# Moving the magnitude of six w_out pieces to ScalarE and the low part of w_sg to GpSimd

## The chip, the cores and the metric

The kernel runs on one core of one Trainium2 chip. Its time is what the device takes for one execution, in microseconds (us); lower is better. One core has five engines that run side by side, each through a queue of its own, in the order fixed when the program is built: TensorE (PE, the matmuls; its weight loads are shown as PEld), VectorE (DVE), ScalarE (ACT), GpSimd (POOL) and SyncE (SP, which here issues nearly all DMAs). An instruction that waits holds up everything behind it in its queue.

## The reference

Three layers follow one another, for 4 batches of 576 rows and 512 columns:

```
scores = q k^T / 8 + slope_h * -(|i - j|), kept where 0 <= i - j < 128;  x = softmax(scores) v   (8 heads of 64)
h = gelu(x @ w_in);  u, v = halves of h
v_n = (v - mean) / sqrt(var + 1e-6) * g_ln
x2 = x + (u * (w_sg @ v_n + b_sg)) @ w_out            (w_sg is 576 x 576, over the rows; w_out 512 x 512)
h = relu(x2 @ w_in2); c = convolution of h over 3 rows; out = (h * sigmoid(c)) @ w_out2
```

Some inputs (w_in, w_out, w_in2, w_out2, the convolution's weights) come as 64-bit floats, w_sg as 32-bit floats.

## The kernel before, in words

Every matmul of the dense layers is made of three: each operand is split into a high part (the value cast to the matmul's own format) and a low part (the value minus the high part), and high x high, high x low and low x high are summed in PSUM. So each weight is prepared in SBUF before it is used.

A 64-bit weight is first turned into 32 bits by whole-number work in `narrowed` (L310). The load brings pairs of words. For a piece of 128 x 256 numbers the steps are: the magnitude of the high word into a tile `wa` (on VectorE a bitwise AND at L324, or on ScalarE the activation Abs at L322, chosen by the argument `act_abs`), a clamp (L328), mask and shift (L329), the sign and top bits (L330), and the bits of the low word (L331), all but the first always on VectorE. Then `split` (L244) makes the high part with `copy` and the low part with `tt`, a subtraction; the table `ON` (L41) names the engines for each kind of operand. For w_out ("wo") the high part is a cast on ScalarE (L222) and the low part a subtraction on GpSimd (L231). There are two `wa` buffers for these pieces, so the third piece starts when the low part of the first is done. The eight pieces are the steps `o0.0` to `o3.1` (function `w_out_piece`, L373).

w_sg comes as five pieces of 128 x 576, steps `g0` to `g4` (function `w_sg_piece`, L363): a cast on ScalarE (L222, "w32 hi") and a subtraction ("w32 lo", L231). Pieces of both kinds are loaded by `staged` (L358) into tiles of a ring of eight buffers with the tag "x"; a load into a used buffer waits until its last reader is done.

The order of the steps is written out by hand (`_steps`, L57). Around the change the first batch's dense layer is woven with the attention of the second batch, whose four head pairs are called p4 to p7 here: `C` scores (matmuls into PSUM, then nine fused bias-and-minimum instructions on VectorE, L451, tile t), `E` exponentials on ScalarE (L186, nine for each pair), `N` the scaling by 1/sum (L242, VectorE or GpSimd; the reciprocal at L498 and L499), `T` transposes on TensorE (L515, tile pT) and their copies to SBUF (tile ph, L222 or L224), `A` the product with v (tile o). Of the dense layer `V` makes v (psv, its statistics at L781 to L786, the vn tiles), `U` makes u (psu), `G` multiplies by w_sg (pss), scales and adds on VectorE (L843), multiplies by u on GpSimd (L231, tile t) and splits the result into gh and gl, and `W` multiplies by w_out (pso). The scores of p4, p5 and p6 and all of `U` come before the first `G`. Six PSUM banks serve the attention; one pair's scores take five.

Some operations may go to one of several engines. A planner decides at build time, in the order of the steps: `load` holds booked nanoseconds of each engine, `book` adds to it, and `pick` takes the engine with the lowest sum; an engine's sum is never lower than 6000 ns behind TensorE's (L39, L202). The costs that it books are those in `copy`, `tt` and `scaled` (L215 to L242). `narrowed` books the same on VectorE whichever engine takes the magnitude. Behind the planner, the framework places each engine's instructions in an order of its own, from the priorities of the steps and a model of their times.

Of the kernel before, what the change touches and what calls it, by code (L numbers as in the profile page):

```python
# [38 lines left out]
SLACK = 6000.0  # L39

ON = {  # L41
    "clamp": "dve", "win hi": "act", "win lo": "pool", "win u hi": "dve", "win u lo": "pool", "w64 hi": "pool", "w64 lo": "pool", "w32 hi": "act", "wo hi": "act", "wo lo": "pool", "w32 lo": "dve",
    "norm": "dve pool",
    "x hi": "act pool", "x lo": "dve", "x first hi": "act", "x first lo": "pool", "x late hi": "act", "x late lo": "dve", "vn first hi": "act", "vn first lo": "dve", "vn hi": "pool", "vn lo": "dve",
    "gate": "pool", "g hi": "act dve pool", "g lo": "dve pool", "x2 hi": "act pool", "x2 lo": "dve",
# [89 lines left out]
def attention_gmlp_glu_kernel(  # L135
# [24 lines left out]
    def f(ap):  # L160
        return ap.bitcast(F32)
# [39 lines left out]
    def book(eng, ns):  # L201
        load[eng] = max(load[eng], load["pe"] - SLACK) + ns  # L202

    def pick(costs):
        eng = min(costs, key=lambda e: max(load[e], load["pe"] - SLACK) + costs[e])
        book(eng, costs[eng])
        return eng
# [36 lines left out]
    def split(hi, lo, src, kind=None, done=None):  # L244

        ins = copy(hi, src, kind is None, ON[kind + " hi"] if kind else "act dve")
        if done is not None:
            done[:] = [ins.ins.name]
        return tt(lo, src, f(hi), ALU.subtract, ON[kind + " lo"] if kind else "dve")
# [9 lines left out]
    with tc.using_default_side("right"):  # L259
        pa = ExitStack()  # L260
        apool = pa.enter_context(tc.tile_pool(name="apool", bufs=2))
# [27 lines left out]
    for i in range(NP):  # L289
        st = cpool.tile([P, 18], F32, name=f"st{i}")  # L290
# [19 lines left out]
    def narrowed(src, n, pool, tag, bufs, spool, stag, sbufs, act_abs=False):  # L310

        if spool is None:
            st = src
        else:
            st = spool.tile([P, STAGE[stag]], U32, tag=stag, name="w64", bufs=sbufs)
            dma = nc.sync.dma_start(st[:, : 2 * n], src)
            later(dma)
        words = st[:, : 2 * n].rearrange("p (n w) -> p n w", w=2)
        low, high = words[:, :, 0], words[:, :, 1]
        a = pool.tile([P, 256 if tag == "wa" else 512], U32, tag=tag, name="wa", bufs=bufs)[:, :n]  # L320
        if act_abs:
            tc.keep_in_program_order(nc.scalar.activation(f(a), f(high), AF.Abs))  # L322
        else:
            ins = tc.keep_in_program_order(nc.vector.tensor_scalar(a, high, 0x7FFFFFFF, None, op0=ALU.bitwise_and))  # L324
            if last_hi:
                tc.add_manual_dep(ins.ins, last_hi[-1], follow, reason="high part first")
        clamp = nc.gpsimd if pick({e: c for e, c in dict(dve=67 + 0.52 * n, pool=147 + 0.93 * n).items() if e in ON["clamp"]}) == "pool" else nc.vector
        tc.keep_in_program_order(clamp.tensor_scalar(f(a), f(a), W_LOW, W_HIGH, op0=ALU.max, op1=ALU.min))  # L328
        nc.vector.tensor_scalar(a, a, 0x07FFFFFF, 3, op0=ALU.bitwise_and, op1=ALU.logical_shift_left)  # L329
        nc.vector.scalar_tensor_tensor(a, high, 0xC0000000, a, op0=ALU.bitwise_and, op1=ALU.bitwise_or)  # L330
        nc.vector.scalar_tensor_tensor(a, low, 29, a, op0=ALU.logical_shift_right, op1=ALU.bitwise_or)  # L331
        book("dve", 200 + 2.6 * n)
        return f(a)

    def cols(w, k, c0, n):

        return w.bitcast(U32)[:, k, 2 * c0 : 2 * (c0 + n)]

    w64, last_in, last_win, last_hi = {}, [], [], []

    def later(dma):

        tc.add_manual_dep(dma.ins, last_in[0].ins.name, follow, reason="later")
# [14 lines left out]
    def staged(src, dtype):  # L358
        st = mpool.tile([P, S], dtype, tag="x", name="wst", bufs=8)[:, : src.shape[-1]]
        later(nc.sync.dma_start(st, src))  # L360
        return st
# [11 lines left out]
    def w_out_piece(k, half):  # L373
        if k == half == 0:
            kept["wo"] = w1pool.tile([P, NK, 2, 2, 256], F32R, tag="wo", name="wo")
        st = staged(cols(w_out, k, half * 256, 256), U32)
        a = narrowed(st, 256, apool, "wa", 2, None, "x", 8)
        split(kept["wo"][:, k, half, 0, :], kept["wo"][:, k, half, 1, :], a, "wo")

    p2pool = []  # L380
# [491 lines left out]
    def constants(i):  # L872
# [11 lines left out]
        B=rotations,  # L884
        k=constants, l=z_load, v=z_vload, c=z_scores, e=z_exp, n=z_norm, t=z_transpose, z=z_av, j=w_in_load, L=a_load, M=a_vload, C=a_scores, E=a_exp, N=a_norm, T=a_transpose, A=a_av,
        X=a_xsplit, V=m_v, U=m_u, G=m_sg, W=m_wo, i=w_in_piece, g=w_sg_piece, o=w_out_piece, a=w2_piece,
    )

# [230 lines left out]
```

## Time and profile before

| what | value |
|---|---|
| median of 3 runs | 543.01 us (542.52 to 544.82) |
| the profiled execution's own time | 543.29 us |
| its span, first to last instruction | 541.1 us |
| matrix multiplies and weight loads (PE, PEld) | 520.7 us and 474.7 us busy |
| VectorE, ScalarE, GpSimd busy | 367.7, 258.7 and 243.2 us |
| granted TensorE clock, mean | 0.997 |

The profile is of one execution, and 2.2 us of its time lie outside the span. Busy time of an engine is summed over its instructions; what is left of the span is idle, and each idle stretch is put down to the instruction that ended it (its releaser). Matmuls are pipelined, so a busy TensorE can still be slowed. The granted clock is a share of full speed: 1.00 is 2.4 GHz and 0.50 is 1.2 GHz.

### The profile page before, as it was taken

The numbers are of one execution on the slowest core, as the hardware profiler recorded it, in microseconds if no ns is written. First come the engines' busy times: TensorE is split into PE (matmuls) and PEld (weight loads), VectorE is DVE, ScalarE is ACT, GpSimd is POOL, SyncE is SP. The second block draws the span as 40 slices with busy tenths as digits, with TensorE's granted clock in tenths as the row PEclk, the third lists the DMA queues.
The fourth block names the chain that finished last, engine by engine and source line by source line (L and its number), as shares of the span: only waits on it lengthen the run. The fifth ranks groups of instructions, "written<-read, shape, count | busy, mean of one in ns | idle before, by whom it ended". The sixth has DMA issues, their size and how long they took to land.

```text
span 541.1 us, 11980 instructions
## 1 busy us (share of the span) xinstructions
PE 520.7 (96%) x4548; PEld 474.7 (88%) x4548; DVE 367.7 (68%) x959; ACT 258.7 (48%) x673; POOL 243.2 (45%) x383
## 2 busy tenths in 40 slices
PE   8997989999998999999999999999999999999997
PEld 6776879898898988989988999998998999999887
DVE  4999798754878875879767688687567354654300
ACT  6694578342458451376534434452554333444310
POOL 2444238542146363246453344245586545465500
PEclk9999989999999999999999999999999999999999
DMA  8974541433261765243643433902202100100011
GB/s 290 394 241 175 150 121 52 148 113 98 89 201 37 218 187 190 82 124 92 173 144 115 155 101 131 337 13 52 75 21 81 66 22 19 42 21 27 33 39 59
DMA packets 33209, 63.93 MB, mean 118 GB/s; under 512 B 3968, under 2 KB 13952, under 8 KB 33152
## 3 DMA queue, kind: packets, MB, share of 16 engines
q1 hardware_dynamic: 33008, 63.04, 35.8%
q8 instruction: 36, 0.59, 0.5%
q14 instruction: 21, 0.17, 0.1%
q10 hardware_dynamic: 144, 0.13, 0.1%
HBM read 48.47 MB, written 14.68 MB: 117 GB/s over the span
## 4 chain that ended last, share of the span: by engine, by line
PE 62%; DVE 14%; ACT 9%; POOL 7%; DMA 5%; issue 3%; SPq 0%; ACTq 0%; DVEq 0%; POOLq 0%
PE psg L213 31%; PE psv L213 7%; PE pso L213 6%; PE psu L213 5%; PE o L213 4%; ACT t L186 3%; PE pss L213 3%; PE sc L213 3%; POOL t L242 3%; PE pT L515 2%; DMA w<-in_w_in_dram 2%; DVE t L451 1%; DVE wa L330 1%; DMA kq<-in_qk_dram 1%; DVE wa L328 1%
## 5 line engine op out<-in xcount | busy, mean ns | idle before, releaser
L213 PEld LDWEIGHTS psg<-x2g,w 128*128 128x128 f32 x768 | 103.1, 188 | 2.4 <-ACT hb L973 0.7
L213 PE MATMUL psg<-x2g,w 128*128 128x256 f32 (+1 forms) x768 | 104.6, 294 | 0.6 <-ACT hb L973 0.5
L213 PE MATMUL psg<-wout,gh 128*128 128x512 f32 (+1 forms) x272 | 80.1, 378 | 0.0
L186 ACT ACTIVATE t<-t,st 128x192 f32<-128x192 f32 (+1 forms) x144 | 61.9, 431 | 15.0 <-DVE st L451 15.0
L213 PE MATMUL pss<-wsg,vn 128*128 128x256 f32 (+1 forms) x448 | 63.6, 298 | 3.6 <-DVE t L843 3.0
L213 PEld LDWEIGHTS pss<-wsg,vn 128*128 128x128 f32 x448 | 60.5, 190 | 4.7 <-DVE t L843 4.0
L977 DVE SCALAR_TENSOR_TENSOR cc<-hb,cw,cc 128x576 f32<-128x576 f32 x32 | 26.6, 832 | 46.9 <-POOL cc L242 46.9
L213 PEld LDWEIGHTS psg<-wout,gh 128*128 128x128 f32 x272 | 49.8, 188 | 8.7
L213 PE MATMUL psu<-xg,win 128*128 128x320 f32 (+1 forms) x384 | 54.2, 298 | 2.6 <-ACT win L222 1.7
L213 PEld LDWEIGHTS psu<-xg,win 128*128 128x128 f32 x384 | 51.7, 188 | 3.7 <-ACT win L222 1.8
L213 PE MATMUL pso<-gh,wo 128*128 128x256 f32 (+1 forms) x256 | 51.8, 300 | 0.5 <-DVE t L843 0.5
L213 PE MATMUL psg<-wout,gl 128*128 128x512 f32 (+1 forms) x136 | 50.9, 378 | 0.0
L213 PE MATMUL psv<-win,xg 128*128 128x512 f32 x192 | 47.6, 398 | 0.9 <-DVE wa L328 0.9
L242 POOL TENSOR_SCALAR cc<-hb,cw 128x576 f32<-128x576 f32 x32 | 28.3, 885 | 42.7 <-ACT hb L973 42.7
L451 DVE CUSTOM_DVE_ANT_0 t<-sc,tab 128x192 f32<-128x192 f32 (+1 forms) x144 | 40.4, 335 | 5.4 <-PE sc L213 5.0
L973 ACT ACTIVATE hb<-psg 128x576 f32<-128x576 f32 x32 | 20.7, 651 | 47.5 <-PE psg L213 45.0
L213 PEld LDWEIGHTS psv<-win,xg 128*128 128x128 f32 x192 | 35.5, 188 | 8.7 <-ACT win L222 1.0
L231 DVE TENSOR_TENSOR gg<-cc,hb 128x576 f32<-128x576 f32 x32 | 30.1, 943 | 17.2 <-ACT cc L186 17.0
L213 PEld LDWEIGHTS pso<-gh,wo 128*128 128x128 f32 x256 | 40.3, 188 | 1.7 <-DVE t L843 1.2
L213 PE MATMUL pso<-gl,wo 128*128 128x256 f32 (+1 forms) x128 | 36.9, 301 | 1.3 <-POOL gl L231 0.6
L231 POOL TENSOR_TENSOR t<-t,u 128x256 f32<-128x256 f32 (+1 forms) x32 | 27.2, 854 | 18.6 <-DVE t L843 18.4
L231 POOL TENSOR_TENSOR gl<-gg,gh 128x512 fp32r<-128x512 f32 x24 | 33.7, 1404 | 0.6
(101 smaller groups left out, 960.4 us busy)
## 6 DMA issues: line engine op xcount, KB each, us to landing
V<-in_v_dram SPq DMA_DIRECT2D x12, 704.0 KB, 4.7
x2s<-x2d SPq DMA_DIRECT2D x16, 288.0 KB, 2.9
w<-in_w_in_dram SPq DMA_DIRECT2D x8, 512.0 KB, 7.5
w<-in_w_out_dram SPq DMA_DIRECT2D x16, 256.0 KB, 3.2
w<-in_w_in_dram SPq DMA_DIRECT2D x16, 256.0 KB, 2.8
wout<-w2d SPq DMA_DIRECT2D x8, 512.0 KB, 6.0
q<-in_q_dram SPq DMA_DIRECT2D x12, 320.0 KB, 4.0
out_dram<-ot SPq DMA_DIRECT2D x15, 256.0 KB, 2.0
```

The costliest lines, as they stand in the source:

```text
L186: ins = nc.scalar.activation(*args, **kw)
L213: return nc.tensor.matmul(out, lhsT, rhs, start=start, stop=stop, **kw)
L231: return (nc.vector if eng == "dve" else nc.gpsimd).tensor_tensor(dst, a, b, op=op)
L242: e.tensor_scalar(dst, src, col, 1.0, op0=ALU.mult, op1=ALU.mult)
L328: tc.keep_in_program_order(clamp.tensor_scalar(f(a), f(a), W_LOW, W_HIGH, op0=ALU.max, op1=ALU.min))
L330: nc.vector.scalar_tensor_tensor(a, high, 0xC0000000, a, op0=ALU.bitwise_and, op1=ALU.bitwise_or)
L451: nc.vector.tensor_tensor_reduce(e, bank, table, scale=-SCALE, scalar=3e38, op0=ALU.add, op1=ALU.min, accum_out=mx)
L515: ins = nc.tensor.transpose(ps[:, i * P : (i + 1) * P], src, ident)
L973: nc.scalar.activation(h[:, 1 : S + 1], ps[:, 256 : 256 + S], AF.Relu)
L977: nc.vector.scalar_tensor_tensor(cc, h[:, 0:S], cw[:, 0, c : c + 1], cc, op0=ALU.mult, op1=ALU.add)
```

## The change

The low parts of the five w_sg pieces are subtracted on GpSimd in place of VectorE, and for the first six of the eight w_out pieces the magnitude is the activation Abs on ScalarE in place of the bitwise AND on VectorE. Nothing else in the source differs; what the planner books for w_sg's low part follows the engine (L229).

```diff
 ON = {
-    ... "wo hi": "act", "wo lo": "pool", "w32 lo": "dve",
+    ... "wo hi": "act", "wo lo": "pool", "w32 lo": "pool",
...
     def w_out_piece(k, half):
...
         st = staged(cols(w_out, k, half * 256, 256), U32)
-        a = narrowed(st, 256, apool, "wa", 2, None, "x", 8)
+        a = narrowed(st, 256, apool, "wa", 2, None, "x", 8, 2 * k + half < 6)
         split(kept["wo"][:, k, half, 0, :], kept["wo"][:, k, half, 1, :], a, "wo")
```

## Rows read from the trace of the kernel before

**Rows 1.** The page's first part: busy us, share of the span, instructions.
```profile
PE 520.7 (96%) x4548; PEld 474.7 (88%) x4548; DVE 367.7 (68%) x959; ACT 258.7 (48%) x673; POOL 243.2 (45%) x383
```
**Rows 2.** Waits of TensorE, 65 to 130 us: total us, times, longest.
```profile
PE sc L213 <- DVE st L451: 2.1, 1, 2.1
PE pso L213 <- POOL gl L231: 0.6, 2, 0.3
```
**Rows 3.** Timeline of TensorE: start, us, line, operation, count [idle before <-releaser].
```profile
50.88 0.38 PE L213 MATMUL psu<-xg,win 128*128 128x256 f32 x1 [1.71 <-ACT win L222]
...
76.77 2.49 PE L213 MATMUL sc<-k,q 64*64 64x192 f32 x24 [2.09 <-DVE st L451]
78.80 10.24 PE L213 MATMUL pss<-wsg,vn 128*128 128x256 f32 x70
88.88 1.58 PE L515 MATMUL pT<-ident,t 128*128 128x128 f32 x13
...
92.44 2.05 PE L213 MATMUL o<-ph,V 128*64 128x64 f32 x52
```
**Rows 4.** Busy us by stretch: PE, PEld, DVE, ACT, POOL, granted clock, DMA.
```profile
50.00:55.00 5.00, 4.12 (x23) 3.63 (x24) 4.35 (x8) 1.63 (x3) 2.16 (x2) 1.00 0.00 0
...
76.70:78.40 1.70, 1.63 (x23) 1.54 (x23) 1.70 (x11) 1.70 (x9) 0.00 (x0) 0.50 0.57 208
78.40:80.10 1.70, 1.70 (x7) 1.70 (x8) 1.67 (x8) 1.70 (x9) 0.26 (x1) 0.50 0.00 0
```
**Rows 5.** Instructions by tile: count, ns min/median/max; the last by form: busy, mean ns.
```profile
L231 DVE TENSOR_TENSOR wsg<-wst,wsg x5: 741/750/759, 56.4 to 67.2; 128x576 fp32r<-128x576 f32 x5
L324 DVE TENSOR_SCALAR wa<-wst x8: 274/288/810, 59.0 to 93.6; 128x256 uint32<-128x256 uint32 x8
L322 ACT ACTIVATE wa<-w x17: 424/438/686, 12.9 to 332.3; 128x256 f32<-128x256 f32 x12, 128x512 f32<-128x512 f32 x5
L231 POOL TENSOR_TENSOR gl<-gg,gh 128x512 fp32r<-128x512 f32 x24 | 33.7, 1404 | 0.6
```
**Rows 6.** Timeline of VectorE from the fourth w_sg piece to the last low parts of vn.
```profile
60.67 0.76 DVE L231 TENSOR_TENSOR wsg<-wst,wsg 128x576 fp32r<-128x576 f32 x1 [0.73 <-ACT wsg L222]
...
73.95 0.28 DVE L324 TENSOR_SCALAR wa<-wst 128x256 uint32<-128x256 uint32 x1
74.26 1.80 DVE L231 TENSOR_TENSOR vn<-v,vn 64x512 fp32r<-64x512 f32 x2
```
**Rows 7.** Timelines of GpSimd and VectorE around 51 us, over one another.
```profile
50.91 1.49 POOL L231 TENSOR_TENSOR win<-wa,win 128x512 fp32r<-128x512 f32 x1 [2.50 <-ACT win L222]
...
48.30 0.43 DVE L329 TENSOR_SCALAR wa<-wa 128x512 uint32<-128x512 uint32 x1
...
51.28 1.40 DVE L329 TENSOR_SCALAR wa<-wa 128x512 uint32<-128x512 uint32 x1
```
**Rows 8.** Timeline of SyncE: the load of the fourth w_sg piece.
```profile
57.17 0.33 SPq L360 DMA_DIRECT2D wst<-in_w_sg_dram  x1
```
**Rows 9.** Timeline of ScalarE: an Abs, the table load, first and last of 27 exponentials.
```profile
27.60 0.64 ACT L322 ACTIVATE wa<-w 128x512 f32<-128x512 f32 x1
...
74.66 1.28 ACT L186 ACT_TABLE_LOAD   x1
75.96 0.40 ACT L186 ACTIVATE t<-t,st 128x128 f32<-128x128 f32 x1
...
88.51 0.45 ACT L186 ACTIVATE t<-t,st 128x192 f32<-128x192 f32 x1
...
89.52 1.74 ACT L222 COPY ph<-pT 128x512 f32<-128x512 f32 x4 [0.17 <-PE pT L515]
```
**Rows 10.** Timeline of GpSimd, 82 to 100 us: scaling and low parts of the gate.
```profile
82.74 4.20 POOL L242 TENSOR_SCALAR t<-t,r 128x128 f32<-128x128 f32 x9 [1.42 <-DVE r L499]
...
89.44 2.71 POOL L242 TENSOR_SCALAR t<-t,r 128x128 f32<-128x128 f32 x7
...
96.73 2.54 POOL L231 TENSOR_TENSOR gl<-t,gh 128x256 fp32r<-128x256 f32 x3
```

More of the change, by code (lines that the diff above doesn't have):

```diff
@@ L41 @@
 ON = {
-    "clamp": "dve", "win hi": "act", "win lo": "pool", "win u hi": "dve", "win u lo": "pool", "w64 hi": "pool", "w64 lo": "pool", "w32 hi": "act", "wo hi": "act", "wo lo": "pool", "w32 lo": "dve",
+    "clamp": "dve", "win hi": "act", "win lo": "pool", "win u hi": "dve", "win u lo": "pool", "w64 hi": "pool", "w64 lo": "pool", "w32 hi": "act", "wo hi": "act", "wo lo": "pool", "w32 lo": "pool",
     "norm": "dve pool",
```

## The prediction

> **What bounds the kernel now.** I read the page's first part, then TensorE's waits, then TensorE's timeline around the longest of them, and from there the queues of the engines that it waits for. TensorE is busy for 520.7 of 541.1 us [rows 1], so all its gaps together are 20.4 us, and work taken from another engine pays only where it closes one of them. VectorE at 68% and ScalarE at 48% bound nothing on the average; the change acts on one stretch, from about 55 us (first w_sg piece) to about 100 us (end of the last w_out piece). In that stretch one gap is long: at 74.68 the scores of p6 stop for 2.09 us for a PSUM bank that VectorE has not yet emptied [rows 3]. The bank comes free with the sixth of the nine masks (L451) of p5, and these stand in VectorE's queue behind pieces of w_sg, w_out and vn. The gap has a second price: when TensorE starts again, its granted clock is 0.50, the 1.2 GHz level, until 80.1 [rows 4], with 1.63 and 1.70 us busy in the two stretches. The gap of 1.71 us at 49.17 [rows 3] was followed by no such fall: the stretch around it stands at 1.00 [rows 4]. A last, small limit comes before 100 us, 0.6 us of waiting for low parts of the gate from GpSimd [rows 2], whose queue is full of scalings and subtractions there [rows 10].
>
> **What leaves VectorE.** Five subtractions at 0.750 us and six magnitudes at 0.284 us [rows 5]: 3.75 + 1.70 = 5.45 us. Ahead of the bank that TensorE misses, and behind 60 us, lie two of the subtractions (at 60.67 and the last, at 67.2), three magnitudes (the last at 73.95) and an idle 0.73 us in which VectorE waited for ScalarE's cast [rows 5, 6]: 1.50 + 0.85 + 0.73 = 3.1 us. The three earlier subtractions and the first magnitude, 2.5 us, I count at nothing, since that wait followed them and would have taken up their time; if it had not, they add to the cover.
>
> **What it costs on GpSimd.** The trace has no 128x576 subtraction on GpSimd. The nearest row, 128x512, is 1.404 us [rows 5]; times 576/512 that is an estimate of 1.58 us, and 7.9 us for five. GpSimd has little to do before 70 us, and its own time is hidden: the matmuls that read w_sg begin at 78.80, at the earliest near 76, and the last subtraction ended on VectorE at about 68; five times 0.83 us (1.58 - 0.75) later is 72.2. If that cover were gone, the first group of `G` would be late by what goes beyond it. Two more things hang on these instructions. A buffer of the staging ring comes free 0.83 us later each time, and SyncE's queue, in order, holds the load of the fourth piece at 57.17 [rows 8], then w_out pieces and the k and q of a later pair; as all are read many microseconds later I take nothing, with 0.8 to 4.2 us of delay to be absorbed. And vn's 1/sqrt(var) runs on GpSimd (L784, L785): behind a subtraction it can be up to 1.58 us late, while VectorE's L786 waits with the masks queued behind it. I take nothing here, as the subtractions are over by about 66 to 68 us when the last two statistics are ready; the upper end is 1.58.
>
> **What it costs VectorE back.** A whole-number instruction of 128x512 took 0.43 us with GpSimd idle and 1.40 us when it met a GpSimd subtraction that had begun 0.37 us before [rows 7]: 0.97 us lost in one meeting. Five new subtractions give 0 to 4.9 us, two of them in the stretch behind 60 us 0 to 1.9 us. I take 1.0 us there, the middle, since about half of VectorE's work in that stretch are masks from PSUM, not pairs of SBUF tiles. That leaves 3.1 - 1.0 = 2.1 us, just the gap of 2.09. The Trainium skill, page SBUF — State Buffer, section Who interferes with whom, goes further against the change: VectorE and GpSimd share a pair of ports, and whichever issues first keeps it for the whole instruction while the other blocks fully. By that rule a meeting costs up to the length of the subtraction, so the estimate would be 7.9 us lost for 5.45 saved; the trace agrees as far as it goes, for VectorE's instruction ended at 52.68, 0.28 us behind GpSimd's end at 52.40 [rows 7].
>
> **What it costs on ScalarE.** An Abs of 128x256 takes about 0.43 us (0.424 the least of the rows, which mix widths) [rows 5], six take 2.6 us. Abs stood between exponentials with no table load [rows 9], so none is added. Three of the six fall before 74 us, where ScalarE has room. The other three fall into 75.96 to 88.96 us, where it runs 27 exponentials without a break, behind a table load that the last gelu of `U` holds at 74.66 [rows 9]. That gelu follows TensorE, which the change does not move before the gap. So the exponentials of p6 end 3 x 0.43 = 1.3 us later, at 90.2.
>
> **What the planner does with it.** Each w_sg piece books 147 + 2.1 x 576 = 1357 ns on GpSimd in place of 67 + 1.045 x 576 = 669 on VectorE. Carried through the steps, GpSimd's sum is soon back at its floor, 6000 ns behind TensorE's, while VectorE's stays 5 x 669 = 3345 ns lower until it reaches its own. So some later choices flip: the low part of the gate for the fourth block of the first half goes from GpSimd to VectorE, four of p5's nine scalings too, p4's last two copies of transposes go from ScalarE to VectorE, and one later low part goes back to GpSimd. On GpSimd's full stretch [rows 10] that takes 4 x 0.47 (4.20 / 9) + 0.85 (2.54 / 3) = 2.7 us away. VectorE gets at most 1.9 + 0.85 + 0.9 (two of four copies in 1.74 us, [rows 9]) = 3.6 us of it in 85 to 99 us; two of these stand ahead of p4's product.
>
> **The sum.** The gap closes: 2.09. The clock stays up: half of 1.63 + 1.70, 1.67. So TensorE stands 3.8 us earlier, and would reach p4's transposes at 85.1 in place of 88.88 [rows 3]. What is late next is attention. p4's exponentials end near 80.3 (9 of 27 in 13.0 us), 81.1 with two Abs, the reciprocal and nine scalings (4.20) give 85.7: 0.6 us late. Then p4's product, at 92.44 before, needs the transposes' copies. If ScalarE makes its two behind all the exponentials, they end at 90.2 + 0.9 = 91.1, and the gain there is 1.3; if it makes them between exponentials, 3.8. The order is not in the trace; I take the middle, 2.6 us. The 0.6 us of GpSimd's low parts I count neither way: its chain is 2.7 us shorter, VectorE's longer. Behind 100 us TensorE has little idle time and carries the difference to the end. The profiled execution took 543.29 us, 0.28 above the median; from the median, 543.0 - 2.6 = 540.4 us, and for this case alone 539.2 to 541.7.
>
> **Rivals.** *All of it stays*: copies between exponentials, GpSimd's shorter chain closing its wait too, 3.8 + 0.6 = 4.4 us, 538.6. For it: transposes have a raised priority in the code. Against: ScalarE is full to 90.2. *The meetings eat it*: five of 0.97 us are 4.9 of the 5.45 us, the sixth mask comes no earlier than about 76, the gap and the low clock stay, 543.0 (542.3 to 543.6). For it: [rows 7]; against it: VectorE meets only what its queue holds at that time. The Trainium skill's rule on the shared ports (page SBUF — State Buffer) leads here. *Abs comes late*: VectorE's L328 of the fourth w_out piece stands ahead of p5's sixth mask and waits for an Abs that ScalarE has queued behind the table load and exponentials. It decides from the point where that Abs ends later than 76.6, when the mask ended before; behind five exponentials it ends at 75.96 + 5 x 0.48 + 0.43 = 78.8, the gap is 2.2 us longer and the low clock follows it: 545.2. For it: ScalarE has no idle time there; against it: the piece's load and buffer are there by 73.95 [rows 6], before the table load. That the code does not do what it says can't be: both edits select a branch that the trace already shows in other pieces.
>
> **How the numbers follow.** Forecast 0.42, all of it 0.18, meetings 0.26, late Abs 0.14. A difference below 0.5% (2.7 us) can't be told from none. Faster by more: half of the forecast's range and the first rival, 0.39; slower by more: 0.13; the rest, 0.48. The range leaves out most of the late Abs and the best part of the first rival: 538.2 to 544.2.
>
> **What would show it.** Right: no gap of 2 us in TensorE ahead of `G`, no stretch at 0.50 there, `G` starting near 76, five subtractions of about 1.6 us on GpSimd, six Abs of 0.43 on ScalarE, p4's product 1.3 to 3.8 us earlier. Wrong: VectorE instructions of over 1 us beside the subtractions, L328 waiting for ScalarE, or a framework that orders the queues anew and opens a gap elsewhere.

## The result: slower by 1.4%, and the profile after

| | before | after |
|---|---|---|
| median | 544.87 us (6 runs, 542.52 to 547.20) | 552.48 us (6 runs, 549.56 to 555.23) |
| profiled execution, span | 543.29 us, 541.1 us | 549.56 us, 547.7 us |
| from p4's first scores to the third batch's first scores | 71.84 us | 78.39 us |

The ratio is 1.0142, with a 95% interval of 1.0109 to 1.0176. The forecast was 540.4 us with a range up to 544.2: wrong in sign and size. The third line of the table, called *the stretch* below, holds 6.55 of the 6.6 us by which the span grew. It also leaves out what happens ahead of 60 us, where some of the profiled executions below have one more low clock.

The page's first part, after (TensorE's busy time is nearly that of [rows 1], so the loss is idle time and clock):
```profile
PE 521.7 (95%) x4548; PEld 476.2 (87%) x4548; DVE 367.9 (67%) x954; ACT 259.7 (47%) x677; POOL 247.9 (45%) x384
```
TensorE in the stretch, kernel before (busy us, granted clock, DMA share, GB/s):
```profile
59.78:131.62 71.84, 68.41 (x737) 0.98 0.38 121
```
The same of the kernel after, and under it the two parts with a low clock:
```profile
59.71:138.10 78.39, 69.59 (x737) 0.93 0.36 114
84.53:89.76 5.23, 5.22 (x24) 0.50 0.00 0
100.41:103.36 2.95, 2.95 (x46) 0.50 0.02 6
```
The same 737 matmuls: idle time grew from 3.43 to 8.80 us, and busy time by 1.18 us; 8.2 us were run at 0.50, the 1.2 GHz level, where it was 3.4 us before [rows 4].

TensorE's timeline after (start, us, line, operation, count, idle before and releaser):
```profile
75.08 1.42 PE L213 MATMUL sc<-k,q 64*64 64x192 f32 x24 [0.68 <-DVE st L451]
76.20 3.93 PE L213 MATMUL pss<-wsg,vn 128*128 128x256 f32 x28
84.53 9.86 PE L213 MATMUL pss<-wsg,vn 128*128 128x256 f32 x55 [4.41 <-DVE t L843]
94.23 1.58 PE L515 MATMUL pT<-ident,t 128*128 128x128 f32 x13
...
100.41 3.42 PE L213 MATMUL o<-ph,V 128*64 128x64 f32 x52 [3.65 <-issue]
```
Against [rows 3]: the gap ahead of p6's last scores is 0.68 us where it was 2.09, and no low clock follows it. `G` begins at 76.20 where it was 78.80. So far the prediction holds. Then come two gaps that were not there, 4.41 us inside `G` and 3.65 us ahead of p4's product, each followed by a low clock (0.50). p4's transposes come 5.4 us later than before, p7's scores (112.40; 105.92 before) 6.5.

ScalarE's timeline after, ahead of the first gap:
```profile
76.14 0.41 ACT L222 CAST wo<-wa 128x256 fp32r<-128x256 f32 x1 [3.08 <-DVE wa L331]
...
77.39 0.43 ACT L322 ACTIVATE wa<-wst 128x256 f32<-128x256 f32 x1 [0.51 <-POOL wo L231]
77.73 0.42 ACT L186 ACTIVATE u<-psu 128x320 f32<-128x320 f32 x1
78.17 1.28 ACT L186 ACT_TABLE_LOAD   x1
```
The same cast in the kernel before:
```profile
73.57 0.41 ACT L222 CAST wo<-wa 128x256 fp32r<-128x256 f32 x1 [0.20 <-DVE wa L331]
```
VectorE's, up to the second gap:
```profile
57.36 0.69 DVE L781 BATCH_NORM_STATS2 bs<-v 128x6 f32<-128x512 f32 x1 [3.05 <-ACT v L186]
...
64.83 1.52 DVE L231 TENSOR_TENSOR vn<-v,vn 128x512 fp32r<-128x512 f32 x1 [0.19 <-ACT vn L222]
66.27 0.28 DVE L328 TENSOR_SCALAR wa<-wa 128x256 f32<-128x256 f32 x1
...
75.69 0.42 DVE L331 SCALAR_TENSOR_TENSOR wa<-wst,wa 128x256 uint32<-128x256 uint32 x1
76.91 0.59 DVE L328 TENSOR_SCALAR wa<-wa 128x256 f32<-128x256 f32 x1 [0.81 <-ACT wa L322]
...
83.75 0.35 DVE L498 TENSOR_SCALAR r<-st 128x9 f32<-128x9 f32 x1 [1.68 <-ACT t L186]
84.01 0.47 DVE L843 SCALAR_TENSOR_TENSOR t<-pss,gln,bsg 128x256 f32<-128x256 f32 x1
...
96.03 0.86 DVE L498 TENSOR_SCALAR r<-st 128x9 f32<-128x9 f32 x1
...
97.18 2.33 DVE L242 TENSOR_SCALAR t<-t,r 128x128 f32<-128x128 f32 x5
99.43 0.87 DVE L224 COPY ph<-pT 128x512 f32<-128x512 f32 x2
```
Read backwards from the first gap: TensorE waits for L843, which empties a bank of the first `G`. L843 (84.01) stands in VectorE's queue behind p4's reciprocal step L498, which waited 1.68 us for the last of p4's exponentials. These began at 79.47 (75.96 in [rows 9]), behind the table load at 78.17 (74.66). The table load follows `U`'s last gelu, and that stands behind the third w_out piece's cast (76.14), which waited 3.08 us for VectorE's L331 (75.69), itself behind five of p5's masks. Two Abs follow the cast (76.45 and 77.39), and the second waited 0.51 us for a `wa` buffer. The cast begins 2.57 us later than before, the table load 3.51; the Abs and their wait lie in the rest. VectorE's first instruction of a w_out piece, L328, begins at 66.27; before, its L324 began at 58.99. And VectorE, which was to be relieved, sat idle for 3.05 and 2.16 us ahead of 57.36 and 60.43. For the second gap the profile names no engine ("issue"), but p4's last two copies, now on VectorE, end at 100.30, 0.11 us before TensorE starts; they stand behind p6's reciprocal (96.03) and five scalings (97.18).

GpSimd's timeline after, first and last of the five subtractions, and vn's 1/sqrt(var) (tile rs) between them:
```profile
56.33 4.20 POOL L231 TENSOR_TENSOR wsg<-wst,wsg 128x576 fp32r<-128x576 f32 x3
60.61 0.19 POOL L784 TENSOR_SCALAR rs<-ba 128x1 f32<-128x1 f32 x1
...
62.67 0.55 POOL L785 TENSOR_TENSOR rs<-rs,mhalf 128x1 f32<-128x1 f32 x1
...
64.36 1.44 POOL L231 TENSOR_TENSOR wsg<-wst,wsg 128x576 fp32r<-128x576 f32 x1 [0.51 <-ACT wsg L222]
```
They take 1.40 to 1.44 us (4.20 / 3 for the first three; the estimate was 1.58), and were done at 65.8. The six Abs took 0.42 to 0.45.

One thing more stands in that queue. The statistic of vn was ready on VectorE at 58.27, but its 1/sqrt(var) began at 60.61, behind the third subtraction, and its second step at 62.67, behind the fourth. It was done at 63.22, 4.95 us after the statistic; before, 0.98 us after it (60.34). VectorE's L786, the cast of vn and vn's low part (64.83) follow, and L328 stands behind that low part.

### The profile page after: what moved, and what is told of

The parts are those of the page before. It is cut to its first block, busy times and chain, and to the rows that moved or that the text cites. A ratio compares the mean times of both kernels' runs of the same rounds, so it can differ in the third digit from the quotient of the medians.

```text
span 547.7 us, 11979 instructions
## 1 busy us (share of the span) xinstructions
PE 521.7 (95%) x4548; PEld 476.2 (87%) x4548; DVE 367.9 (67%) x954; ACT 259.7 (47%) x677; POOL 247.9 (45%) x384
## 4 chain that ended last, share of the span: by engine, by line
PE 59%; DVE 14%; ACT 11%; POOL 7%; issue 5%; DMA 3%; SPq 0%; POOLq 0%; ACTq 0%
PE psg L213 30%; PE pso L213 7%; ACT t L186 5%; PE psv L213 5%; PE psu L213 5%; PE pss L213 4%; PE o L213 4%; PE sc L213 3%; PE pT L515 2%; DVE wa L330 2%; DVE wa L329 1%; POOL t L242 1%; DVE wa L328 1%; DMA w<-in_w_in_dram 1%; ACT gh L222 1%
## 5 line engine op out<-in xcount | busy, mean ns | idle before, releaser
L213 PE MATMUL pss<-wsg,vn 128*128 128x256 f32 (+1 forms) x448 | 65.3, 304 | 8.2 <-DVE t L843 7.3
L213 PEld LDWEIGHTS pss<-wsg,vn 128*128 128x128 f32 x448 | 62.2, 195 | 9.3 <-DVE t L843 8.0
L451 DVE CUSTOM_DVE_ANT_0 t<-sc,tab 128x192 f32<-128x192 f32 (+1 forms) x144 | 40.4, 335 | 5.4 <-PE sc L213 4.5
```

Of the source, the lines that this page charges most:

```text
L213: return nc.tensor.matmul(out, lhsT, rhs, start=start, stop=stop, **kw)
L451: nc.vector.tensor_tensor_reduce(e, bank, table, scale=-SCALE, scalar=3e38, op0=ALU.add, op1=ALU.min, accum_out=mx)
```

## Experiments

Two accounts at first. *Order*: the framework lays ScalarE's and VectorE's queues out anew, and the cast ahead of the last gelu is the cause. *Planner*: the choices that flip with the 1357 ns booked on GpSimd are the cause. The rivals of the prediction, late Abs and port meetings, stay in play. Ratios are to the kernel before, run on the same chip, with 95% intervals.

**Which half.** The Abs alone:

```diff
-    ... "w32 lo": "pool",
+    ... "w32 lo": "dve",
```


> Only the six Abs on ScalarE; the low parts of w_sg stay on VectorE. Queue theory (the exponentials of p4 start late because instructions that wait stand ahead of the last gelu in ScalarE's queue, and the reciprocal of p4 stands ahead of the first L843 in VectorE's): two Abs that wait for a wa buffer still stand ahead of the last two gelus, so the table load comes at 76.5 to 78.5 us in place of 74.66, TensorE has a gap of 1 to 4 us at the first group of G; no second gap before p4's product, since the planner's choices are those of before; time 2 to 7 us above before. Port theory (GpSimd's five subtractions stall VectorE): nothing is left of the loss, time as before or up to 2 us below.

Measured: 543.92 us, 0.999 (0.9953 to 1.0027). The queue theory missed here: the table load came at 74.99, not at 76.5 to 78.5, and no loss is measured. The subtractions on GpSimd alone:

```diff
-        a = narrowed(st, 256, apool, "wa", 2, None, "x", 8, 2 * k + half < 6)
+        a = narrowed(st, 256, apool, "wa", 2, None, "x", 8)
```


> Only the low parts of w_sg on GpSimd; all eight magnitudes stay on VectorE. Queue theory: the cast of the third w_out piece still stands ahead of the last gelu and waits for VectorE's L331, so the table load is late by 2 to 3 us (77 us) and the first gap is 2 to 4 us; the planner's flips are in, so two copies of p4's transposes are on VectorE and the second gap before p4's product stays at 2 to 4 us; time 5 to 9 us above before. If the Abs alone are the cause: table load at about 74.7, no first gap, time 1 to 3 us below before. Port theory: as the changed kernel, with VectorE instructions of over 1 us beside each subtraction.

Measured: 551.72 us, 1.011 (1.0077 to 1.0144). Half the Abs:

```diff
-        a = narrowed(st, 256, apool, "wa", 2, None, "x", 8, 2 * k + half < 6)
+        a = narrowed(st, 256, apool, "wa", 2, None, "x", 8, 2 * k + half < 3)
```

> The change with Abs for the first three w_out pieces alone. Queue theory: the two Abs ahead of the last gelu are gone (0.43 + 0.51 wait + 0.43 = 1.3 us), the cast of the third piece stays ahead of it; table load at about 76.9 in place of 78.17, first gap 3 us in place of 4.4, the second gap as in the changed kernel; time 1 to 3 us below the changed kernel. If the Abs alone are the cause: table load at 74.7, no first gap, time 5 to 7 us below the changed kernel.

Measured: 549.46 us, 1.0098 (1.0065 to 1.0130); the gap inside `G` is 3.80 us. By themselves the six Abs cost nothing that can be measured, and with no Abs moved at all the loss is nearly whole, so "late Abs" falls as its cause. Behind the late cast they do cost something: from p4's first scores to the table load it is 18.46 us with six Abs (the changed kernel) and 17.68 with three. The planner's flips are in both of the last two kernels, yet p4's product waits 0.86 us with three Abs and not at all with none, where p5's product waits 2.42 us for its copies: the flips alone do not fix where the second gap is. ScalarE's timeline of the kernel with the subtractions alone shows the same late cast ahead of gelu and table load:
```profile
77.34 0.41 ACT L222 CAST wo<-wa 128x256 fp32r<-128x256 f32 x1 [2.01 <-DVE wa L331]
...
78.10 1.28 ACT L186 ACT_TABLE_LOAD   x1
```

**Planner or order.** GpSimd makes the subtractions, but the planner is told the old cost on VectorE:

```diff
-        tt(lo, st, f(hi), ALU.subtract, ON["w32 lo"])
+        book("dve", 67 + 1.045 * width(st)); nc.gpsimd.tensor_tensor(lo, st, f(hi), op=ALU.subtract)
```


> The change with the planner told the old cost (669 ns on VectorE for each w_sg piece), so that its later choices are those of before. Planner theory for the second gap: p4's copies are on ScalarE again, the gap of 3.65 us before p4's product and the low clock behind it go (3.65 + about 1.5), the first gap of 4.4 us stays; time 4 to 5 us below the changed kernel, 2 to 4 above before. If the choices are not the cause of the second gap: time as the changed kernel.

Measured: 548.13 us, 1.005 (1.002 to 1.008). The first gap stays (4.41 us), the second falls from 3.65 to 0.99:
```profile
101.25 2.04 PE L213 MATMUL o<-ph,V 128*64 128x64 f32 x52 [0.99 <-ACT ph L222]
```
The other way about, the planner as it is, but the third cast and the fourth to sixth Abs ordered behind p4's first exponential (`instrs` maps names to instructions, `casts` and `magnitudes` hold those of the w_out pieces):

```diff
+            ex = act(e, e, AF.Exp, ...); (b, m, j, i) == (1, 0, 1, 0) and [tc.add_manual_dep(x, ex.ins.name, follow, reason="exp first") for x in [instrs[casts[2]]] + magnitudes[3:]]
```


> The change with one order added on ScalarE: the cast of the third w_out piece and the Abs of the fourth to sixth stand behind p4's first exponential, so nothing that waits for VectorE stands ahead of the last gelu and the table load. Queue theory: table load at 74 to 75 us in place of 78.17, p4's reciprocal near 81 in place of 83.75, the first gap 1 to 2 us in place of 4.41, and TensorE's clock stays at 1.00 behind it; the planner's flips and the second gap stay; time 4 to 7 us below the changed kernel. Rival (VectorE's own queue, which holds p6's masks and w_out work ahead of the first L843, sets the gap whatever ScalarE does): first gap stays over 3 us, time within 2 us of the changed kernel.

Measured: 548.71 us, 1.0088 (1.0063 to 1.0113), some 3 us below the changed kernel, where 4 to 7 were expected. Its ScalarE has the table load back early:
```profile
74.24 1.28 ACT L186 ACT_TABLE_LOAD   x1
...
76.60 0.41 ACT L222 CAST wo<-wa 128x256 fp32r<-128x256 f32 x1 [0.57 <-DVE wa L331]
```
and its TensorE loses 1.25 us at that place, but then 1.88 and 2.04, after which the clock is low (0.50 in 101 to 104 us):
```profile
81.50 5.88 PE L213 MATMUL pss<-wsg,vn 128*128 128x256 f32 x42 [1.25 <-DVE t L843]
...
97.50 0.51 PE L213 MATMUL pso<-gh,wo 128*128 128x256 f32 x2 [1.88 <-DVE t L843]
...
100.96 0.80 PE L213 MATMUL pso<-gh,wo 128*128 128x256 f32 x2 [2.04 <-ACT wo L222]
```
Both edits at once:

> Both at once: ScalarE's order as in the run with late casts and the planner told the old cost. If the two gaps have the two causes and these add: 8 to 11 us below the changed kernel, that is as before or up to 3 us below it. If the loss of the changed kernel has a third cause (GpSimd's subtractions against VectorE): still 3 us or more above before.

Measured: 546.37 us, 1.0036 (1.0010 to 1.0061). The four kernels make a table, in which both causes show (the stretch is of one profiled execution each):

| stretch, ratio | planner as changed | planner told the old cost |
|---|---|---|
| third cast ahead of the gelu | 78.39 us, 1.0142 | 75.23 us, 1.0050 |
| third cast and fourth to sixth Abs behind p4's first exponential | 76.95 us, 1.0088 | 72.30 us, 1.0036 |

The planner's choices are worth 3.2 and 4.7 us of the stretch, the order on ScalarE 1.4 and 2.9; both together 6.1 of 6.55. The edit moves the Abs together with the cast, so the table does not tell the two apart. The times show less than the stretch: with both edits 0.36% is left of 1.42%, about 2 us and clear of noise. What is left goes with the granted clock, whose mean was 0.999 in the profiled execution (544.00 us) and 0.990 to 0.994 in six of the ten (546.09 to 548.30 us); no trace shows where it fell in these. One choice of the planner by itself, p4's two copies kept on ScalarE:

```diff
-            last = pick(dict(act=640, dve=740))
+            last = pick(dict(act=640, dve=740)) if (b, m) != (1, 0) else "act"
```


> The change with p4's last two copies of transposes forced back to ScalarE; the other flips of the planner stay. If those copies behind p6's reciprocal and five scalings on VectorE are the second gap: it falls from 3.65 us to 1 us or less, time 3 to 5 us below the changed kernel. If the four scalings and the low part moved to VectorE are the cause: gap and time as in the changed kernel.

Measured: 549.74 us, 1.0101 (1.0080 to 1.0123), the second gap 1.24 in place of 3.65 us, though p5's product then waits 1.86 for its own copies on VectorE:
```profile
98.42 2.04 PE L213 MATMUL o<-ph,V 128*64 128x64 f32 x52 [1.24 <-ACT ph L222]
```
Last, the flips with nothing moved: the kernel before, with the planner told GpSimd's cost for a subtraction that VectorE makes:

```diff
-        tt(lo, st, f(hi), ALU.subtract, ON["w32 lo"])
+        book("pool", 147 + 2.1 * width(st)); nc.vector.tensor_tensor(lo, st, f(hi), op=ALU.subtract)
```


> The kernel before with every engine of w_sg and w_out as it was, but the planner is told the new cost (1357 ns on GpSimd for each w_sg piece). So only the flips are in: four scalings and a low part of the gate to VectorE, two copies of p4's transposes from ScalarE to VectorE. Planner theory, flips costly by themselves: a gap of 1 to 4 us before p4's product, 2 to 5 us above before. If the flips cost only where p4's exponentials are late already: within 1.5 us of before.

Measured: 547.56 us, 1.0066 (1.0041 to 1.0091). No instruction is made elsewhere but those that the planner chose, and 3.6 us are lost. Its TensorE keeps the gap of 2.09 and gets two more, for a scaling of `G` and a copy of p5's transposes, both on VectorE; the gap that was expected before p4's product did not come (p4's first scores are 2.5 us late here, with a low clock at 50 to 60 us):
```profile
79.54 1.45 PE L213 MATMUL sc<-k,q 64*64 64x192 f32 x24 [2.09 <-DVE st L451]
...
101.61 0.50 PE L213 MATMUL pso<-gh,wo 128*128 128x256 f32 x2 [1.43 <-DVE t L843]
...
104.95 2.05 PE L213 MATMUL o<-ph,V 128*64 128x64 f32 x52 [0.84 <-DVE ph L224]
```
Its stretch is 73.30 us, 1.5 longer than before, and the span behind the stretch 1.4 longer, with a new wait of 1.29 us at 247.98 for L843 in the next batch.

**Why VectorE's w_out pieces begin late.** In the kernels so far with the subtractions on GpSimd the first L328 begins 6.6 to 7.5 us after p4's first scores; with them on VectorE, 0.2 to 0.8 us ahead of these scores. In the source L328 is kept behind what was traced last on its engine. Before, that was a w_sg subtraction; now it is the low part of vn, which ended at 66.35, and which came behind the 1/sqrt(var) that GpSimd's subtractions held up. No run took that wait away, so how much of the delay it makes is open. First the pin was taken from the w_out pieces (`pin` stands for it in `narrowed`):

```diff
-        a = narrowed(st, 256, apool, "wa", 2, None, "x", 8, 2 * k + half < 6)
+        a = narrowed(st, 256, apool, "wa", 2, None, "x", 8, 2 * k + half < 6, pin=lambda ins: ins)
```

> The change, but the first two VectorE steps and the Abs of a w_out piece are no longer pinned behind the instruction traced last on their engine. In the kernel before that was the low part of a w_sg piece; with these on GpSimd it became a low part of vn, about 7 us later. Pin theory: the first w_out piece is worked on by 60 us again in place of 66.3, the casts reach ScalarE before the gelus wait for them, table load by 75 us, first gap 2 us or less; time 3 to 7 us below the changed kernel. Rival: the pins only set an order that VectorE's load gives anyway; time within 2 us of the changed kernel.

Measured: 550.64 us, 1.0130 (1.0096 to 1.0163). L328 began 1.3 us after p4's scores (64.29), but took 1.38 us, and its piece's L331 came only at 70.69; casts still waited ahead of the last gelu, and the gap was 4.54. Without the pin the framework spread the piece's steps out. Its time says little about the pin, though: its stretch is 74.32 us, 4.1 shorter than the changed kernel's, and p4's product does not wait, but p4's first scores come 3.2 us later than before (62.96). Unpinned, an Abs of w_out stood ahead of an earlier table load and waited for its own DMA, and TensorE then waited 2.01 us, up to 42.16:
```profile
39.77 0.43 ACT L322 ACTIVATE wa<-wst 128x256 f32<-128x256 f32 x1 [2.15 <-DMA wst<-in_w_out_dram]
40.22 1.28 ACT L186 ACT_TABLE_LOAD   x1
```
So the neighbour was changed instead, by tracing the first piece ahead of the third part of v:

```diff
-            uv = ["g0", "g1", V[2], "g2", "o0.0", U[0][3], "g3", "o0.1", V[4]] + ...
+            uv = ["g0", "g1", "g2", "o0.0", V[2], U[0][3], "g3", "o0.1", V[4]] + ...
```


> The changed kernel with one step moved: the first w_out piece is traced ahead of the third part of v (order g0 g1 g2 o0.0 V2 in place of g0 g1 V2 g2 o0.0). Account A, the neighbour in the program: each clamp L328 of a w_out piece is kept behind what was traced last on VectorE. Before, that was a w_sg subtraction at 58; with the subtraction gone to GpSimd it is the low part of vn at 64.8, so all of VectorE's w_out work begins 7 us late and the third cast, which stands ahead of the last gelu in either kernel, is late. Then here L328 begins near 59 in place of 66.3, the third cast ends by 74.5, the table load is at 74 to 75 in place of 78.2, the gap ahead of the second part of G falls from 4.4 to under 1.7 us without the 1.2 GHz stretch; what the planner's other choices cost stays: about 548.5 (ratio 1.007 to 1.010). Account B, the place of the clamp is no cause (GpSimd's subtractions themselves, or the framework's model, make the casts late): table load stays near 78, the gap near 4.4, ratio 1.012 to 1.016.

Measured: 546.98 us, 1.0060 (1.0034 to 1.0086). VectorE and GpSimd of this kernel:
```profile
58.00 1.51 DVE L328 TENSOR_SCALAR wa<-wa 128x256 f32<-128x256 f32 x1 [3.42 <-ACT wa L322]
59.55 1.40 DVE L329 TENSOR_SCALAR wa<-wa 128x256 uint32<-128x256 uint32 x1
...
68.11 0.28 DVE L328 TENSOR_SCALAR wa<-wa 128x256 f32<-128x256 f32 x1
```
```profile
56.57 4.23 POOL L231 TENSOR_TENSOR wsg<-wst,wsg 128x576 fp32r<-128x576 f32 x3
```
The first link holds: L328 begins at 58.00. Two others don't. It took 1.51 us and the next step 1.40, where 0.28 and 0.29 are usual, while GpSimd made three subtractions from 56.57 to 60.80: brought forward, the pieces meet them. And the second piece is now the one behind vn's low part (68.11), so that the fourth cast takes the third's part:
```profile
78.44 0.41 ACT L222 CAST wo<-wa 128x256 fp32r<-128x256 f32 x1 [2.95 <-DVE wa L331]
...
79.21 1.28 ACT L186 ACT_TABLE_LOAD   x1
```
The gap inside `G` is 4.18 us, as account B has it. The time is at the lower end of account A's or below, but by another road: p4's product (98.31) waits for nothing, as its last two copies, still on VectorE, begin at 95.10. The same move with the old cost in the books, and then with L843 ordered ahead as below:

> The same move, and the planner is told the old cost of the w_sg subtraction on VectorE, though GpSimd makes it. Account A with the planner's choices as the other cause: both are gone, and what is left is the relief of VectorE; 541 to 545, ratio 0.996 to 1.002, no gap above 2 us between 70 and 110 us. Account B: the gap of 4.4 stays, 548, ratio 1.005 or more, as with the old cost alone.

> The second of these, and the first L843 (which frees the bank that the second half of G waits for) ordered ahead of p4's reciprocal and p6's last three masks. If the order of VectorE's queue is what still stands between the earlier G and a gain, no wait for L843 at G and 540 to 543.5, ratio 0.993 to 0.999; if ScalarE's copies of p4's transposes, behind 27 exponentials, hold the product at 92 in any case, ratio 0.997 to 1.001 and p4's product waits 1 to 2 us for ScalarE.

Measured: 547.82 us, 1.0066 (1.0036 to 1.0096), gap 4.18; and 547.10 us, 1.0055 (1.0031 to 1.0078), gap 3.98. In this order of the queues the planner's choices cost nothing that can be measured (1.0060 with them, 1.0066 without). As long as a cast that VectorE can't feed in time stands ahead of the last gelu, the gap stays in every run, whichever piece it is. That it shrinks to 1.25 us when the cast and three Abs are put behind an exponential was shown; why the framework puts it ahead was not. It may reckon VectorE's pieces earlier than they run, but its reckoning is in no trace.

**Where the predicted gain went.** With the Abs alone TensorE's timeline is:
```profile
74.92 0.51 PE L213 MATMUL sc<-k,q 64*64 64x192 f32 x2 [0.42 <-DVE st L451]
76.28 1.42 PE L213 MATMUL sc<-k,q 64*64 64x192 f32 x24 [0.85 <-DVE st L451]
...
82.62 5.75 PE L213 MATMUL pss<-wsg,vn 128*128 128x256 f32 x42 [1.63 <-DVE t L843]
...
98.32 0.38 PE L213 MATMUL pso<-gl,wo 128*128 128x256 f32 x1 [1.85 <-POOL gl L231]
```
```profile
60.09:132.15 72.06, 66.60 (x738) 1.00 0.38 120
```
The clock stays up (busy time 1.81 us less than before), the 2.09 us became 0.42 + 0.85, and 1.63 us are lost at the first L843, 0.43 for ScalarE's copies and 1.85 for GpSimd's low parts: idle 5.46 in place of 3.43 us. So I ordered the first L843 ahead of p4's reciprocal and p6's last three masks, in that kernel, in it with the planner's flips (and p4's copies on ScalarE), and in the changed kernel with both causes removed:

(`behind_l843` holds the reciprocal's L498 and the three masks)

```diff
+        st = nc.vector.scalar_tensor_tensor(t1, ...); (b, half, d) == (0, 0, 0) and [tc.add_manual_dep(x, st.ins.name, follow, reason="L843 first") for x in behind_l843]
```


> The six Abs alone (w_sg's low parts on VectorE) with the first L843 ahead of p4's reciprocal and p6's last three masks. In the run with Abs alone the first gap was 1.63 us, with the clock at 1.00, and the wait for GpSimd's low part of the gate 1.85 us. If VectorE's order sets the first gap: it falls below 0.5 us. If GpSimd's full stretch of 82 to 98 us sets the end: the wait for its low part grows by what is won, and the time stays as before; if not, 1 to 2 us below before.

> The same with GpSimd relieved in its full stretch: the planner is told the new cost, so that four scalings and a low part of the gate go to VectorE, while p4's copies are held on ScalarE. If GpSimd's stretch was what gave the gain back: its wait (1.85 us) is gone and the time is 2 to 3.5 us below before. If ScalarE's exponentials and VectorE's copies bound it: within 1 us of before.

> The change with late casts and the old books, and one order more: the first L843 stands ahead of p4's reciprocal and of p6's last three masks in VectorE's queue. If VectorE's order is what is left of the first gap: it falls from 1.25 us to 0.5 or less, and TensorE reaches p4's transposes at 86.5 or sooner; whether time follows depends on the waits behind, for copies and for L843 at 97 to 100 us. Theory that ScalarE's 27 exponentials bound p4's product: product at 91 to 92.5 us all the same, time within 1 us of the run without this order. Theory that the gap is all: 1 to 2 us below before.

Measured: 543.33 us, 0.9995 (0.9967 to 1.0024); 545.27 us, 1.0030 (0.9999 to 1.0061); 544.87 us, 0.9986 (0.9956 to 1.0015). The first two keep VectorE's subtractions; the flips cost some 0.35% there. The last has the whole change in it, without the late cast and the flips, and is the best that it came to: no difference that can be measured. Its TensorE, p4's copies on its ScalarE, and its stretch:
```profile
75.44 1.41 PE L213 MATMUL sc<-k,q 64*64 64x192 f32 x24 [0.91 <-DVE st L451]
...
92.23 2.04 PE L213 MATMUL o<-ph,V 128*64 128x64 f32 x52 [1.73 <-ACT ph L222]
```
```profile
90.19 1.04 ACT L222 COPY ph<-pT 128x512 f32<-128x512 f32 x2
...
91.44 0.74 ACT L222 COPY ph<-pT 128x512 f32<-128x512 f32 x2
```
```profile
59.82:131.28 71.46, 66.56 (x738) 1.00 0.39 125
```
Nothing is lost at `G`, yet p4's product starts at 92.23 where it started at 92.44 [rows 3]: it waits 1.73 us for copies that end at 92.18, after the exponentials (to 89.64), two casts and an Abs. The stretch is 0.38 us shorter than before.

## Why the prediction was wrong, by its steps

- **What leaves VectorE, and the gap ahead of `G`**: came out. The gap went from 2.09 to 0.68 us, the clock stayed up, and `G` began at 76.20 where "near 76" was forecast. Part of that is luck, since VectorE's queue had been laid out anew and the sum was worked out for the old one. With the Abs alone the waits there are 0.82 us less; 0.85 was forecast for three magnitudes. TensorE's busy time fell by 1.81 us there; 1.67 was forecast for the clock.
- **GpSimd's subtractions and ScalarE's Abs**: 1.44 us against an estimate of 1.58, and 0.43 as forecast; hidden from the matmuls that read w_sg, as said.
- **"vn's 1/sqrt(var) ... I take nothing here"**: mis-sized. The reason looked at the last two statistics alone. The first of the three was ready at 58.27 and met the subtractions: its 1/sqrt(var) was done at 63.22, where it had been at 60.34, 2.9 us later (the upper end was 1.58). VectorE's w_out pieces stand behind what follows from it; what that is worth was not tested.
- **Port meetings**: small after the change: vn's low part took 1.52 us where it took 0.68, a loss of 0.84; the masks (L451, out of PSUM) beside the fourth subtraction took 0.27 to 0.34, as before. VectorE's w_out pieces had moved away from the subtractions; in the kernel with the first piece put back, two instructions lost 1.23 and 1.12 us. The Trainium skill's rule (page SBUF — State Buffer, section Who interferes with whom: the one that issues first keeps the shared ports for its whole instruction) fits the second of these: it ended at 60.95, GpSimd's third subtraction at 60.80. (The row of 0.43 us in [rows 7] was not all with GpSimd idle, as the prediction reads it: an instruction there ended at 48.42.)
- **"That gelu follows TensorE, which the change does not move before the gap."** This step failed. In both kernels the third cast stands ahead of the gelu; before, it waited 0.20 us for VectorE, and the gelu followed TensorE closely (`U` ended at 73.47, the last gelus began at 73.89). The change made VectorE's w_out pieces begin 7 us later, the cast waited 3.08 us, two of the Abs came between it and the gelu and not behind the table load as forecast, and the table load went from 74.66 to 78.17. The prediction followed VectorE's time up to the missing bank, and not what else VectorE feeds. Putting that cast and the last three Abs behind an exponential is worth 1.4 to 2.9 us of the stretch.
- **"What is late next is attention", 0.6 us**: attention was late by the table load, through a queue that the prediction had not read on: L843 behind L498. With the Abs alone, where the table load is early, L843 still came at 82.09, hardly earlier than before (82.55), behind p6's masks and the reciprocal, and TensorE lost 1.63 us there.
- **"What the planner does with it"**: the flips were found rightly, and valued with the wrong sign: 2.7 us off GpSimd were counted as relief or nothing. They cost 3.2 us of the stretch in the changed kernel, and alone, in the kernel before, 0.66%; with the first piece moved they cost nothing that can be measured. The copies were priced as 0.9 us of work; what they cost in the changed kernel is their place, behind p6's reciprocal and scalings, 2.4 of the 3.65 us of the second gap.
- **The middle between 1.3 and 3.8 us of gain**: not reached even with all of this undone. p4's product started 0.2 us earlier; the lower end, copies behind all the exponentials, was nearly it.
- **The rivals**: "late Abs" had the queue and the price of a slower case, but the wrong instruction: L328 did wait 0.81 us for an Abs (76.91), behind the masks that freed the bank. The case that happened stood only in the last line of what would make it wrong, a framework that orders the queues anew, and had no price and no chance of its own.

## What to carry to other kernels

Where the framework lays the queues out, moving an operation to another engine moves its neighbours too: list every instruction that is pinned behind it, queued behind it on its new engine or booked after it, and ask of each consumer on the other engines what stands behind it there. Price a flip of the planner by its place in the new queue, not by its length; telling the planner the old cost, or the new cost without the move, separates the two in one run each. When a gap on TensorE closes, look at once for the next instruction that empties a bank.

## What the runs showed of the hardware

The clock does not follow from the length of a gap alone. After the gap of 1.71 us at 49 to 51 us it stayed at 1.00 in the kernels before and after, and fell in others: 0.66 over 50 to 60 us in the profiled executions of the kernels with only the planner's cost changed and with the old cost. With the Abs alone, gaps of 0.42 and 0.85 us were followed by 1.00; with L843 ordered first as well, gaps of 0.52 and 0.85 us were followed by 0.68 over 80 to 85 us. So a few tenths of a per cent between two of these kernels are not read from one profile.
